# Attention and experts on one core: experts half a step later, order from token lists, value loads first

## The chip, the cores and the metric

One core of one Trainium2 chip. The metric is the time of one execution in microseconds (us), on the device. A kernel is executed several times, its figure is the median, and the profile is of one of those executions; the span that a profile names is 1.6 to 1.7 us shorter than that execution's time. Most executions agree within a per cent; those over 1.5% above the fastest of the same kernel count as slow and stay out of all ratios.

Engine names: PE is TensorE's matmul, PEld its weight load, DVE VectorE, ACT ScalarE, POOL GpSimd, SP the engine that issues most DMA transfers. A bracket such as `[5.14 <-DVE early L464]` says that the engine sat idle for 5.14 us until DVE's work on tile `early` (line 464) was done.

## The reference, cut to what matters

```python
# attention: B=8, H=8, S=576, D=64
s_pos = np.maximum(s, 0.0)
cum = np.cumsum(s_pos, axis=-1)
bias = -(cum[:, :, :, None] - cum[:, :, None, :])          # a decay
scores = np.where(causal, -1e9, scores + np.minimum(bias, 0.0))
attn = softmax(scores);  x = attn @ v                      # (B, S, 512)
# experts: E=8, F=1024, one expert per batch element, top 1
logits = x.mean(axis=1) @ w_gate
e_idx  = np.argmax(logits, axis=1)
h   = np.maximum(x @ w1[e_idx], 0.0)
out = gate_w * (h @ w2[e_idx])
```

The gate needs the mean over all positions of a batch's attention output, and the choice of the expert decides which 2 MB of weights are loaded. So each batch has a chain: last value product, gate matmul, weight load, first expert matmul. The kernel hides it by working on the attention of the next batches meanwhile.

## The kernel before: the parts that matter

A *quad* is four heads of a batch: quads 0 and 1 make batch 0. A *unit* is two heads. Queries and keys come in as fp32, are cast to bf16 on VectorE, transposed on TensorE, and copied out of PSUM by VectorE or ScalarE. GpSimd multiplies the values with the decay.

```python
def cast_qk(n, i):                       # i = 0 query, 1 key (half of the tile)
    src = qk_nat[n][:, i, :, :]
    if n < NEARLY:                       # the first four quads: a plain cast
        qk_bf[n] = early[n]
        nc.vector.tensor_copy(out=qk_bf[n]..., in_=src...)
        return
    ...
    nc.vector.tensor_scalar(             # later quads: the same, and a minimum besides
        out=qk_bf[n]..., in0=src..., scalar1=1.0, scalar2=0.0,
        op0=ALU.mult, op1=ALU.min, accum_out=amin[:, 2*n+i : 2*n+i+1])

def do_vS(n):                            # GpSimd: values times decay
    nc.gpsimd.tensor_tensor(out=dst[:, :, :, 0:D], in0=src, in1=gc..., op=ALU.mult)
    nc.gpsimd.tensor_copy(out=dst[:, :, :, D], in_=gc)
```

The beginning is a hand-written list, the steady part an interleaving computed by budgets:

```python
def begin():
    keep_pe(KEEP0)                       # 11 filler matmuls: keep TensorE's clock up
    cast_qk(0, 0); do_tr_part(0, 0, 0, "a"); do_tr_part(0, 0, 1, "a")
    keep_pe(2); cast_qk(0, 1); ...
    # ... up to the gate of batch 0:
    do_tr_part(3, 0, 0, "v")
    do_vS_pair(2, 0); do_vS_pair(2, 1)   # GpSimd, behind the weight load of batch 0
    load(5, picked[0]); load(6)
    do_scores_masked(4, 0); exp_only(4, 0)
    do_gate2(0)                          # softmax of the gate
    cast_qk(3, 1)                        # VectorE: key of quad 3
    do_tr_part(3, 0, 1, "v"); ...
    do_vS(3)                             # GpSimd again

def emit_all():
    begin()
    for u in range(LAG, END):            # one unit of attention per round
        ...                              # expert quanta placed by weights and budgets
```

## Time and profile before

| | before |
|---|---|
| time, first three runs | 240.71 us median (239.87 to 242.27) |
| span of the profiled run | 240.1 us (that execution took 241.70 us, above the median) |
| first exponential / gate matmul of batch 0 / first expert matmul | 11.5 / 27.1 / 39.4 us |
| starts of the experts of batches 1 to 7 | 63.7, 94.1, 119.8, 146.1, 170.9, 195.1, 216.5 us |
| last expert matmul ends | 233.7 us |

The starts are the times of each batch's first matmul from `xT` and `w_sb` in the timeline. They cut the execution into stretches. Here are VectorE and then GpSimd around 30 us (start, duration, engine, line, operation):

```profile
29.93 0.74 DVE L394 CAST early<-qk_nat 128x1152 bf16<-128x1152 f32 x1
...
31.33 0.24 POOL L454 CAST vS<-g_col 128x10 bf16<-128x10 f32 x1
31.48 1.27 POOL L455 TENSOR_TENSOR vS<-vN,g_col 128x640 bf16<-128x640 f32 x1
```

The cast of quad 3's key takes 0.74 us.

### The profile page before, as it was taken

Reading aid. Unit: us, or ns where it says so; the run is one execution under the profiler, and the core shown is the slowest. Engines: PE = TensorE matmul, PEld = TensorE weight load, DVE = VectorE, ACT = ScalarE, POOL = GpSimd, SP = SyncE. Lnnn points to the kernel's source line nnn. Section 1 sums busy time; section 2 is a strip of 40 time slices with the busy share of each in tenths; the row PEclk is TensorE's granted clock in tenths of the full one; section 3 lists DMA queues with packets and bytes.
Section 4 is the critical chain, followed back from the end, with each engine's and each line's share of the span. In section 5 each row is a group of like instructions: output and inputs, shape, how many; then the busy total and the mean of one; then the engine's idle time right before and its main releaser. Section 6 shows DMA issues by size and latency. Waiting matters only on the chain.

```text
span 240.1 us, 5998 instructions
## 1 busy us (share of the span) xinstructions
PE 214.1 (89%) x2330; PEld 157.1 (65%) x2330; DVE 164.5 (69%) x378; ACT 140.3 (58%) x254; POOL 92.6 (39%) x145
## 2 busy tenths in 40 slices
PE   6597789999999796999899997999999998898990
PEld 2365457875787655867597857776877776557740
DVE  5578768658797784779686875777777544396640
ACT  2588547467656745576648655685658675434330
POOL 6181092018845194308362556218360830100000
PEclk9999859999999999999999999999999999999997
DMA  5999999999999999999999999969921893399222
GB/s 174 342 237 351 306 200 216 344 309 284 221 309 312 286 257 209 304 306 305 225 254 347 313 217 241 337 159 187 228 94 44 162 230 117 67 214 235 82 84 76
DMA packets 55186, 55.14 MB, mean 230 GB/s; under 512 B 39712, under 2 KB 40752, under 8 KB 53104
## 3 DMA queue, kind: packets, MB, share of 16 engines
q1 hardware_dynamic: 52816, 37.91, 51.8%
q0 software_dynamic: 2336, 16.79, 35.4%
q8 instruction: 20, 0.33, 0.5%
q14 instruction: 14, 0.11, 0.2%
HBM read 62.03 MB, written 9.44 MB: 298 GB/s over the span
## 4 chain that ended last, share of the span: by engine, by line
PE 52%; DMA 26%; ACT 7%; DVE 7%; issue 4%; POOLq 1%; SPq 0%; ACTq 0%; POOL 0%; DVEq 0%
DMA w_sb<-in_moe_w_dram 24%; PE mm_ps L655 18%; PE mm_ps L693 13%; PE av_ps L528 6%; PE sc_ps L471 4%; ACT xT L583 4%; PE tr_ps L428 3%; DMA qk_nat<-in_k_dram 2%; ACT pT L501 2%; PE x_ps L580 2%; PE sc_ps L488 1%; PE tr_ps L416 1%; PE lg_ps L617 1%; PE mm_ps L669 1%; POOLq L624 1%
## 5 line engine op out<-in xcount | busy, mean ns | idle before, releaser
L655 PE MATMUL mm_ps<-xT,w_sb 128*128 128x288 bf16 x512 | 74.5, 289 | 4.9 <-DMA w_sb<-in_moe_w_dram 4.4
L501 ACT ACTIVATE pT<-sc_ps 128x1024 bf16<-128x1024 f32 x64 | 62.5, 1021 | 23.5 <-PE sc_ps L471 14.7
L655 PEld LDWEIGHTS <-w_sb 128*128 128x128 bf16 x512 | 61.5, 146 | 9.0 <-DMA w_sb<-in_moe_w_dram 5.1
L693 PE MATMUL mm_ps<-w_sb,hT 128*128 128x512 bf16 x256 | 64.9, 380 | 1.3 <-DMA w_sb<-in_moe_w_dram 0.6
L507 POOL TENSOR_SCALAR_AFFINE_SELECT pT<-pT 128x512 bf16<-128x512 bf16 x50 | 31.5, 638 | 43.8 <-ACT pT L501 43.7
L661 DVE TENSOR_SCALAR hT<-mm_ps 128x288 bf16<-128x288 f32 x64 | 28.7, 454 | 22.0 <-PE mm_ps L655 22.0
L663 ACT ACTIVATE hT<-mm_ps 128x288 bf16<-128x288 f32 x64 | 26.4, 413 | 26.8 <-PE mm_ps L655 26.1
L702 ACT ACTIVATE o_sb<-mm_ps,gw 128x512 f32<-128x512 f32 x32 | 22.1, 691 | 31.2 <-PE mm_ps L693 31.1
L693 PEld LDWEIGHTS <-hT 128*128 128x128 bf16 x256 | 22.8, 98 | 22.1 <-DVE hT L661 2.9
L430 DVE TENSOR_SCALAR_CACHE_REDUCE qkT<-tr_ps 128x1152 bf16<-128x1152 bf16 x24 | 32.5, 1353 | 3.8 <-PE tr_ps L428 3.6
L401 DVE TENSOR_SCALAR_CACHE_REDUCE qk_bf<-qk_nat 128x1152 bf16<-128x1152 f32 x24 | 32.1, 1342 | 0.0
L441 POOL TENSOR_TENSOR vS<-vN,g_col 128x1280 bf16<-128x1280 f32 x13 | 30.3, 2332 | 0.0
L626 POOL DMA_DIRECT2D w_sb<-in_moe_w_dram x8 | 5.2, 645 | 63.1 <-issue 18.7
L528 PEld LDWEIGHTS <-pT 128*128 128x128 bf16 x576 | 22.4, 99 | 4.7 <-ACT pT L501 1.4
L528 PE MATMUL av_ps<-vS,pT 128*128 128x65 bf16 x576 | 23.8, 195 | 1.1 <-ACT pT L501 0.9
L471 PE MATMUL sc_ps<-qkT 64*128 64x256 bf16 (+2 forms) x320 | 21.7, 256 | 1.8 <-ACT qkT L422 1.1
L563 DVE TENSOR_TENSOR x_nat<-av_ps,recip 128x640 bf16<-128x640 f32 x26 | 21.4, 824 | 0.9
L583 ACT ACTIVATE xT<-x_ps 128x576 bf16<-128x576 bf16 x30 | 19.2, 650 | 3.4 <-PE x_ps L580 3.0
L471 PEld LDWEIGHTS <-qkT 64*128 64x128 bf16 x320 | 12.6, 95 | 11.2 <-issue 3.9
L428 PE MATMUL tr_ps<-ident_bf,qk_bf 128*128 128x128 bf16 x216 | 16.0, 219 | 0.1
L428 PEld LDWEIGHTS <-qk_bf 128*128 128x128 bf16 x216 | 13.9, 98 | 3.1 <-DVE qk_bf L401 0.5
L561 DVE RECIPROCAL recip<-av_ps 128x10 f32<-128x10 f32 x26 | 5.7, 220 | 14.0 <-PE av_ps L528 12.9
(92 smaller groups left out, 187.8 us busy)
## 6 DMA issues: line engine op xcount, KB each, us to landing
w_sb<-in_moe_w_dram POOLq DMA_DIRECT2D x16, 1024.0 KB, 12.4
qk_nat<-in_q_dram SPq DMA_DIRECT2D x16, 576.0 KB, 5.6
qk_nat<-in_k_dram SPq DMA_DIRECT2D x16, 576.0 KB, 6.3
vN<-in_v_dram SPq DMA_DIRECT2D x64, 128.0 KB, 5.5
out_dram<-o_sb SPq DMA_DIRECT2D x32, 256.0 KB, 5.7
vN<-in_v_dram SPq DMA_DIRECT2D x16, 64.0 KB, 5.8
out_dram<-o_sb SPq DMA_DIRECT2D x16, 64.0 KB, 4.2
s_nat<-in_s_dram SPq DMA_DIRECT2D x1, 144.0 KB, 2.8
```

Of the source, the lines that this page charges most:

```text
L401: nc.vector.tensor_scalar(out=qk_bf[n][:, i, :, :, :].rearrange("p r hh d -> p hh r d"), in0=src.rearrange("p hh (r d) -> p hh r d", d=D), ...
L428: nc.tensor.transpose(flat[:, r, :], qk_bf[n][:, i, r, :, :], ident_bf)
L430: nc.vector.tensor_scalar(out=tr_out(n, i, 0, R), in0=flat[:, 0:R, :].rearrange("p r (g n) -> p g n r", g=2), scalar1=1.0, scalar2=0.0, op ...
L441: nc.gpsimd.tensor_tensor(out=dst[:, :, :, 0:D], in0=src, in1=gc[:, :, :, None].to_broadcast([P, NT, 4, D]), op=ALU.mult,)
L471: nc.tensor.matmul(sc[:, hh, o : o + W[tj]], src[hh * 64 : hh * 64 + 64, 1, g, tj * P : tj * P + P], src[hh * 64 : hh * 64 + 64, 0, g, tj ...
L501: nc.scalar.activation(out=ph, in_=sc_ps[half], func=AF.Exp, scale=SCALE)
L507: nc.gpsimd.affine_select(out=ap, in_=ap, compare_op=ALU.is_ge, fill=0.0, base=0, pattern=[[0, 4], [1, P]], channel_multiplier=-1,)
L528: nc.tensor.matmul(av[:, ti, :], src[:, o : o + P], vs[:, tj, 2 * hh + u % 2, :], start=(tj == tjs[0]), stop=(tj == tjs[-1]),)
L583: nc.scalar.activation(out=xT[b][:, c, :], in_=flat, func=AF.Copy, accum_out=pooled[b][:, c : c + 1])
L655: nc.tensor.matmul(mm, w1[:, c, ft, :], xT[b][:, c, sc * SC : (sc + 1) * SC], start=(c == 0), stop=(c == NC - 1),)
L661: nc.vector.tensor_scalar_max(out=dst, in0=mm, scalar1=0.0)
L693: nc.tensor.matmul(mm[0:n, :], hT[b][:, fc, st * P : st * P + n], w2[:, fc, :], start=(fc == 0), stop=(fc == NF - 1),)
```

## The change

Its intent: every expert starts half a step later behind its own gate, so that its weights have landed; the order of all engines is no longer computed but read from four lists of tokens, so that it can be tuned place by place; and most value loads of the first quads go out ahead of the later query and key loads.

```diff
+FIRST = """
+L0.0 I L0.1 L1.0 l0.3 l0.1 l3.0 l1.3 l0.0 l1.0 l1.1 L1.1 ...      # loads; I is the load of s
+"""
+BEGIN = """
+k2 C0.0 U0.0.0 u0.0.0.1 U0.0.1 C0.1 J U0.1.0 U0.1.1 ...           # k2: two fillers, were 11
+... g0 C3.1 E4.0 ... U3.1.1 u3.1.1.0 V3 M5.0 ... k6 ... k1 A6 H0.0.1 ...
+... Y0.1.0 V4 x1.3.1 P1.3 H0.1.3 G1 ... m1 ... O0.0 l6.0 L7.0 l7.1 l6.4 y0.1.0 l7.0 ...
+"""
+PERIOD = """
+... P3.1 G3 O1.2 y2.0.0 m3 ... A16 a16 Y2.1.0 T9.1 t9.1 ...       # shifted by i and repeated
+"""
+FINISH = """
+... O7.2 O7.1 Y7.3.0 Y7.3.1 y7.3.1 Z7 y7.4.2 O7.3 D O7.4.2        # D: the guard, now last
+"""
+    def play(text, shift=0):
+        for word in text.split():
+            args = [int(a) for a in word[1:].split(".") if a]
+            if shift:
+                args[0] += shift * STEP[word[0]]
+            ...
+            OPS[word[0]](*args)
 # ... begin(), the budgets and the queue of quanta are gone ...
+    def sum_mm(j):        # N: gate of batch 0 from column sums of the attention output
+        ...
+            nc.tensor.matmul(t, src[0:n, ti, j*P:(j+1)*P], ones_bf[0:n, :], ...)
```

Tokens: `L`/`l` load a query or key / a value part, `C` cast, `U`/`u` transposes of a half and their copy, `T`/`t` the same for a whole one, `J` transposes of the decay, `S`/`M` scores, `E` exponential, `V`/`v` value scaling on GpSimd, `A`/`B` value product, `X`/`x` transposes of the attention output, `G` gate matmul, `m` pick of the expert and weight load, `g` gate softmax, `H`/`h` first expert layer and its output, `Y`/`y` second, `O` store, `k` fillers. The last digit of `u`, `h`, `y` is the engine (0 VectorE, 1 ScalarE). Letters not named here are smaller steps of the same parts.

## The prediction

> **What bounds the kernel now.** I read the page first: the engine shares and the 40 slices.
>
> ```profile
> span 240.1 us, 5998 instructions
> ...
> PE 214.1 (89%) x2330; PEld 157.1 (65%) x2330; DVE 164.5 (69%) x378; ACT 140.3 (58%) x254; POOL 92.6 (39%) x145
> ...
> PEclk9999859999999999999999999999999999999997
> DMA  5999999999999999999999999969921893399222
> ```
>
> TensorE is the fullest engine, but a busy PE slice is not a full PE, so I do not use 89% as the distance to the floor. The clock drops to half near slice 6 (30 to 36 us). The DMA engines are full until about 165 us. Next come the stretches between the starts of the experts of batches 2, 3, 4 and 5, which the chain of waits places at 94.1, 119.8, 146.1 and 171.0:
>
> ```profile
> 20.00:30.00 10.00, 7.17 (x103) 5.15 (x99) 7.64 (x27) 6.80 (x13) 0.33 (x1) 0.92 1.08 325
> 30.00:40.00 10.00, 8.91 (x98) 5.85 (x99) 7.29 (x16) 5.65 (x6) 6.61 (x8) 0.74 1.04 207
> ...
> 94.10:119.80 25.70, 24.64 (x282) 18.71 (x282) 19.33 (x43) 15.66 (x31) 11.34 (x17) 1.00 1.03 278
> 119.80:146.10 26.30, 24.69 (x283) 18.77 (x283) 19.34 (x43) 17.10 (x33) 12.57 (x19) 1.00 1.06 277
> 146.10:171.00 24.90, 24.66 (x283) 18.81 (x284) 19.09 (x42) 15.33 (x31) 11.78 (x18) 1.00 0.93 234
> ```
>
> One batch takes 24.9 to 26.3 us. What it must take I get from the chain of waits, where PE runs back to back:
>
> ```profile
> 71.24 1.73 PE mm_ps L693 x8
> 72.97 0.55 PE sc_ps L471 x10
> ...
> 95.28 0.55 PE av_ps L528 x18
> ...
> 96.84 0.50 PE tr_ps L428 x9
> 97.34 1.97 PE mm_ps L655 x16
> ...
> 109.13 10.65 DMA w_sb<-in_moe_w_dram
> 119.83 1.20 PE mm_ps L655 x8
> ...
> 169.43 0.99 PE mm_ps L669 x16
> ...
> 201.55 0.75 PE x_ps L580 x10
> ...
> 205.17 0.40 PE lg_ps L617 x2
> ```
>
> First expert layer 64 x 1.97/16 = 7.88; second 32 x 1.73/8 = 6.92 and its tail 0.99; scores and values 4 x 0.55 each = 4.4; query and key transposes 4 x 0.50 = 2.0; x transposes 20 x 0.075 = 1.5; gate 0.4. Sum 24.1 us a batch, so the three windows hold 1.6, 2.2 and 0.8 us that no matmul needs. The waits of PE and its weight loads name the cause:
>
> ```profile
> PEld L655 <- DMA w_sb<-in_moe_w_dram: 5.1, 4, 2.2
> ...
> PE lg_ps L617 <- DVE glog L609: 4.5, 4, 1.5
> ...
> PE mm_ps L655 <- DMA w_sb<-in_moe_w_dram: 4.4, 4, 2.1
> ```
>
> (The first and third are largely one wait seen on two rows.) The reader should see that experts start when their weights land, four times up to 2.2 us late, and that the gate matmul sits in PE's queue ahead of ready work.
>
> **The whole span as a sum.** Eight batches are 8 x 24.1 = 192.8. The seven units whose mask is added by matmuls take 1.24 us instead of 0.55 (timeline, 10.76 to 12.00): +4.9. The transposes of the decay column and the guard add about 1. Work 198.7. PE's first useful instruction is at 7.3 us (timeline). Its last ends at about 233.7, 6.4 before the end. So 240.1 - 7.3 - 6.4 - 198.7 leaves 27.7 us of bubble. Where: after 94.1 the work left is six batches, 144.6, less what attention is ahead (8 scores, 6 values, 8 transposes, one x and gate: 4.4 + 3.3 + 4.0 + 1.9 = 13.6), plus guard 0.5 = 131.5, done in 139.6: 8.1 of bubble. The other 19.6 lie before 94.1, about 14 of them before the first expert at 39.4.
>
> **What the Trainium skill says.** (1) "TensorE: Matmul & The Clock Gate", Part 1: the HAM clock gate: an idle window of about 3.4 us halves the clock, a busy one restores it. The trace agrees in kind: after the thin stretch at 20 to 30 the granted clock is 0.74 over 30 to 40. (2) "DMA: Bandwidth & Descriptors", Issuing engines are not separate DMA queues: transfers issued from Sync, Scalar and GpSimd interleave on the same 16 engines. It agrees: weights issued by GpSimd need 8.2 to 15.9 us to land (median 12.4), the long ones while the DMA share is over 1. (3) "Perfetto Trace Analysis", Identifying the Most-Contended Engine: matmul busy share is a poor measure of headroom; hence the issue intervals above. (4) The same page, Optimizing Tensor Performance, Matmuls: rotate groups through PSUM banks so evacuation overlaps the next matmuls. Here four banks rotate, and the chain shows 1.38 us of four ACT records emptying x banks ahead of expert matmuls (at 103.60, 129.35, 155.59).
>
> **The change part by part.** PE arithmetic is almost unchanged: the same matmuls, plus four 5-matmul column sums for batch 0 (about 0.1 us each, an estimate from the per-matmul intervals above: +0.4) and 14 filler matmuls in place of 24, of which the first burst shrinks from 11 to 2.
>
> *Experts later.* In the repeated list the gate matmul of a batch is followed, before that batch's first expert matmul, by 3 scores, 3 values, 2 transposes, 7 first-layer groups, 6 half second-layer groups and a tail: 1.65 + 1.65 + 1.0 + 7 x 0.49 + 6 x 0.865 + 0.99 = 13.9 us of PE work. Before, gate to expert took 13.3 us twice and 13.8 once (106.55 to 119.83, 80.58 to 94.08 and 132.30 to 146.07), with the 1 to 2 us wait inside. So the steady weight wait nearly vanishes: about -1.3 us in each of three periods, -4 in all. For batches 1 and 2 I count only 11.0 and 12.0 us of such work: there a wait of 1 to 2 us stays.
>
> *Order.* The four x transposes are emptied by three ACT and one DVE instruction instead of four ACT ones of 0.65 + 0.20; the gate matmul comes two groups after the transposes. About -0.5 a period. First-layer outputs go 13 to ACT and 3 to DVE (were 8 and 8), second-layer outputs 2 to ACT and 3 to DVE (were 5 and 0). From the rows (0.41 ACT, 0.45 DVE, 0.69 for a wide output) DVE moves by -2.3 + 0.8 + about 2 = +0.5 us a batch, from 19.3 to about 19.9 in 24.6: 81%, not a bound.
>
> *Gate of batch 0.* Column sums straight from the attention output replace the wait for four transposes and their copies. Before: last value output at 23.9, gate matmul at 27.1. After: sums, two small DVE steps, gate matmul at about 25.2. Weights issue about 1.8 us sooner; the softmax no longer sits in front of the key cast on DVE at the same point. First expert at about 37 instead of 39.4, including the half step.
>
> *Loads.* Value loads of the first quads move before the second quad's key. 128 KB of 256 B packets takes 0.59 us of 16 engines (512 packets at the 18.4 ns that the records of the trace give), so seven of them push that key by about 4 us, to about 13.5 to 14.5. Before, its cast ran at 13.86: a draw, with up to 0.8 us of loss.
>
> *Filler.* With 2 instead of 11 matmuls before the first data, PE is probably at half clock at 7.3 us. The first nine to eighteen transposes and the first scores then cost about 1 us more on the path to the first exponential.
>
> *Tail.* The last output is split over two engines and its two stores over two queues, saving one issue of about 0.5 us; the guard's DVE chain, now last, takes about 3 us and lies beside a store that takes over 4. -0.4.
>
> Sum of bubbles: before 94.1, 19.6 - 2 (gate, first expert) - 0.5 (batch 1) - 2.5 (batch 2: 30.4 us between the starts of batches 1 and 2 for 26.6 of work becomes about 28) + 0.5 (cold clock and key not already counted) = 15. After, 8.1 - 4 (weights), with the 0.5 a period for x partly the same time, = 4. Then 7.3 + 199.1 + 19 + 6.0 = 231.4 of span, and the timed median lies 0.6 above the profiled span: about 232. The fine separation of matmuls and evacuations can only take more small waits out; I put **231.5**.
>
> **Rivals.** *DMA becomes the bound.* Summing all packet times of the trace gives 209 us of 16 engines, 26 a batch while everything is loaded: more than PE's 24.1. Shares of 1.03 to 1.06 mean about 24.8 us a batch at best. Against it: no cast waits for a query or key load in the steady state, and loads end near 165 while quad 15 is transposed near 180, so 10 to 15 us are in hand. If it holds, periods stay at 25.5 and the time is 236 to 238. *Cold start costs more than filler saved*: half clock to 14 us or a second drop near 30; the page would lose 2 to 3 us, 234. *Same waits under new names*: strict queues put an evacuation behind one not yet ready and PE meets full PSUM banks; 237 to 241. *A tight order*: bubbles fall to 0.3 a period and the start loses 6 us; 225 to 227.
>
> **Range and chances.** The removable part is 27.7 us; I claim 9. Taking out only the weight waits gives about 236, all tight orders 226. So 225.5 to 238. Faster by over 2% means below 235.9: 0.80. Within 2%: 0.16. Slower: 0.04.
>
> **What would show it.** Right: expert starts of batches 2 to 5 at 24.3 to 25.0 apart; PE waiting on expert weights under 4 us in total, all in batches 0 to 2; gate of batch 0 near 25; first expert near 37; granted clock under 1 in the first 10 us. Wrong: casts or value scaling waiting on loads (DMA bound); PE waits on ACT or DVE evacuation beyond 5 us; a half-clock stretch longer than 7 us; or a last period after attention with PE idle for batch 7's weights, for which I count 11.3 us of cover.

## The result

| | before | after |
|---|---|---|
| time | 240.31 us (239.87 to 242.27, 4 runs) | **248.28 us** (248.12 to 250.79, 4 runs) |
| ratio of fast runs | | 1.034 (1.027 to 1.042) |
| first exponential / fifth | 11.5 / 17.1 | 13.1 / 20.0 |
| gate of batch 0 | 27.1 | 27.6 |
| starts of the experts | 39.4, 63.7, 94.1, 119.8, 146.1, 170.9, 195.1, 216.5 | 46.8, 70.8, 102.5, 127.6, 152.7, 180.8, 204.9, 224.3 |
| last expert matmul ends / span | 233.7 / 240.1 | 240.25 / 249.1 |

Slower by 3.4%, where 3.7% faster was predicted. A ratio here is the mean time of one kernel's fast runs over that of the other's fast runs of the same rounds, so it isn't quite the ratio of the medians.

The profiled execution of after was its slowest; the others had spans of 246.5 to 247.5. Its page:

```profile
span 249.1 us, 5975 instructions
...
PE 214.1 (86%) x2317; PEld 159.4 (64%) x2340; DVE 177.1 (71%) x392; ACT 129.3 (52%) x238; POOL 90.4 (36%) x145
...
PE   2698719899899988999999998699999999899960
...
PEclk9999977999999999999999999999999999999997
DMA  6999999918999699989999999999970794399140
```

TensorE is busy for the same 214.1 us as before in a span 9 us longer. VectorE is busy for 12.6 us more, which is more than the re-dealt outputs explain. There is a hole in PE in slice 6 (31 to 37 us) and one in DMA three slices later (50 to 56 us).

Where do the 9.0 us of the span come from? By the stretches: up to the first expert +7.4; batch 0 to batch 2 +1.0 (55.7 against 54.7); batch 2 to batch 6 +1.4 (102.4 against 101.0); batch 6 to the last expert matmul -3.25 (35.35 against 38.6); the tail +2.45 (8.85 against 6.4). These add up to 9.0. The largest part is one event. VectorE, then GpSimd, then TensorE of after:

```profile
31.28 5.75 DVE L464 CAST early<-qk_nat 128x1152 bf16<-128x1152 f32 x1
```

```profile
31.34 0.24 POOL L549 CAST vS<-g_col 128x10 bf16<-128x10 f32 x1
31.50 1.27 POOL L550 TENSOR_TENSOR vS<-vN,g_col 128x640 bf16<-128x640 f32 x1
...
34.09 2.32 POOL L534 TENSOR_TENSOR vS<-vN,g_col 128x1280 bf16<-128x1280 f32 x1
36.36 0.79 POOL L538 CAST vS<-g_col 128x20 bf16<-128x20 f32 x1
```

```profile
37.08 1.14 PE L491 MATMUL tr_ps<-ident_bf,early 128*128 128x128 bf16 x9 [5.14 <-DVE early L464]
```

The same cast of the same bytes took 5.75 us instead of 0.74, and it took them exactly while GpSimd scaled values. TensorE waited 5.14 us for it, and its clock fell, too (granted share 0.50 from 34.0 to 40.8 us). GpSimd began its values at the same time in both kernels (31.33 and 31.34); the cast came at 29.93 in before and at 31.28 in after.

What the change was made for did work. In the waits of PE and PEld in after there is no row with `DMA w_sb` left, where before had 4.4 and 5.1 us, and the 4.5 us of the gate matmul on `glog` are down to 0.6. But the wait for weights wasn't the same in every execution of the old order. Here is the row of the first expert layer (busy us, mean ns, idle us before it and what ended most of it) in before, then in e3, an experiment below whose steady part is that of before:

```profile
L655 PE MATMUL mm_ps<-xT,w_sb 128*128 128x288 bf16 x512 | 74.5, 289 | 4.9 <-DMA w_sb<-in_moe_w_dram 4.4
```

```profile
L655 PE MATMUL mm_ps<-xT,w_sb 128*128 128x288 bf16 x512 | 74.5, 289 | 2.7 <-DMA w_sb<-in_moe_w_dram 2.2
```

Of the 2.2 us in e3 only 0.2 lie ahead of batches 3 to 5, against 2.2 in before. The steady stretches of after (columns: window, length, then busy us of PE, PEld, DVE, ACT, POOL, then granted clock, DMA share, GB/s):

```profile
70.80:102.50 31.70, 28.38 (x340) 20.93 (x340) 27.27 (x59) 18.15 (x30) 18.28 (x28) 1.00 0.97 252
102.50:127.60 25.10, 24.65 (x285) 18.94 (x285) 19.97 (x43) 15.33 (x32) 11.87 (x19) 1.00 1.02 258
127.60:152.70 25.10, 24.64 (x286) 18.93 (x285) 19.97 (x43) 15.34 (x32) 11.88 (x19) 1.00 1.01 256
152.70:180.80 28.10, 24.84 (x286) 19.00 (x286) 19.97 (x43) 15.48 (x32) 11.92 (x19) 1.00 1.03 261
180.80:204.90 24.10, 23.91 (x275) 18.36 (x275) 14.99 (x35) 15.28 (x32) 9.64 (x17) 1.00 0.65 158
```

25.1, 25.1 and 24.1 are what a period takes in every later run of this order. The 28.1 has one stall of 2.8 us in it, TensorE waiting for an output tile whose store was late. It is in no other profile that follows, and the shorter spans of the other executions fit with its absence.

And this is the same kind of row of before for batch 1 to batch 2, to be held against the first of those:

```profile
63.70:94.10 30.40, 26.56 (x320) 20.23 (x320) 23.22 (x51) 19.93 (x35) 14.54 (x24) 1.00 1.05 275
```

After has 20 matmul records more in this stretch and 1.8 us more of busy PE: the new lists have put more attention work there.

### The profile page after: what moved, and what is told of

Same layout as the page of the kernel before. It is cut to its first block, busy times and chain, and to the rows that moved or that the text cites.

```text
span 249.1 us, 5975 instructions
## 1 busy us (share of the span) xinstructions
PE 214.1 (86%) x2317; PEld 159.4 (64%) x2340; DVE 177.1 (71%) x392; ACT 129.3 (52%) x238; POOL 90.4 (36%) x145
## 4 chain that ended last, share of the span: by engine, by line
PE 63%; DVE 15%; DMA 8%; issue 5%; ACT 4%; POOL 2%; SPq 0%; DVEq 0%; ACTq 0%; POOLq 0%
PE mm_ps L832 21%; PE mm_ps L864 17%; DMA out_dram<-o_sb 6%; PE sc_ps L568 5%; PE av_ps L634 5%; PE tr_ps L512 4%; ACT pT L600 3%; PE x_ps L709 3%; DVE early L464 3%; PE mm_ps L893 2%; DVE qkT L519 2%; DMA s_nat<-in_s_dram 2%; PE sc_ps L585 2%; DVE qk_bf L472 2%; PE tr_ps L491 1%
## 5 line engine op out<-in xcount | busy, mean ns | idle before, releaser
L864 PE MATMUL mm_ps<-w_sb,hT 128*128 128x512 bf16 x235 | 59.7, 379 | 2.7 <-DVE hT L844 0.8
L607 POOL TENSOR_SCALAR_AFFINE_SELECT pT<-pT 128x512 bf16<-128x512 bf16 x50 | 31.4, 637 | 53.2 <-ACT pT L600 49.2
L842 ACT ACTIVATE hT<-mm_ps 128x288 bf16<-128x288 f32 x81 | 30.4, 416 | 29.7 <-PE mm_ps L832 29.2
L864 PEld LDWEIGHTS <-hT 128*128 128x128 bf16 x256 | 23.4, 98 | 24.5 <-issue 2.7
L844 DVE TENSOR_SCALAR hT<-mm_ps 128x288 bf16<-128x288 f32 x47 | 20.5, 452 | 17.4 <-PE mm_ps L832 17.2
L880 ACT ACTIVATE o_sb<-mm_ps,gw 128x512 f32<-128x512 f32 (+1 forms) x24 | 14.6, 624 | 23.9 <-PE mm_ps L864 17.8
L568 PE MATMUL sc_ps<-qkT 64*128 64x256 bf16 (+2 forms) x320 | 22.9, 260 | 3.9 <-DVE qkT L519 1.8
L798 POOL DMA_DIRECT2D w_sb<-in_moe_w_dram x8 | 4.6, 579 | 56.2 <-issue 24.0
L568 PEld LDWEIGHTS <-qkT 64*128 64x128 bf16 x320 | 12.9, 96 | 15.3 <-issue 7.9
L512 PEld LDWEIGHTS <-qk_bf 128*128 128x128 bf16 x216 | 13.9, 98 | 4.7 <-DVE qk_bf L472 1.4
L491 PE MATMUL tr_ps<-ident_bf,early 128*128 128x128 bf16 x72 | 7.8, 266 | 9.1 <-DVE early L464 9.1
## 6 DMA issues: line engine op xcount, KB each, us to landing
w_sb<-in_moe_w_dram POOLq DMA_DIRECT2D x16, 1024.0 KB, 11.7
```

The source lines that it names most:

```text
L512: nc.tensor.transpose(flat[:, r, :], qk_bf[n][:, i, r, :, :], ident_bf)
L568: nc.tensor.matmul(sc[:, hh, o : o + W[tj]], src[hh * 64 : hh * 64 + 64, 1, g, tj * P : tj * P + P], src[hh * 64 : hh * 64 + 64, 0, g, tj ...
L607: nc.gpsimd.affine_select(out=ap, in_=ap, compare_op=ALU.is_ge, fill=0.0, base=0, pattern=[[0, 4], [1, P]], channel_multiplier=-1,)
L842: nc.scalar.activation(out=dst, in_=mm, func=AF.Relu)
L864: nc.tensor.matmul(mm[0:n, :], hT[b][:, fc, st * P : st * P + n], w2[:, fc, :], start=(fc == 0), stop=(fc == NF - 1),)
```

## The experiments

Fourteen kernels ran, all correct. The start of each batch's experts and the first gate are from the profiles (s: the profiled execution was a slow one); the ratio is against before in the same rounds, and a cell is blank where the argument makes no use of it.

| run | what | median us | ratio of fast runs (95%) | gate 0 | first expert | tail |
|---|---|---|---|---|---|---|
| after | the change | 248.28 | 1.034 (1.027 to 1.042) | 27.6 | 46.8 | 8.85 |
| e1 | that cast in the form with a minimum | 245.05 | 1.013 (1.003 to 1.023) | | 41.6 s | |
| e2 | that cast earlier | 245.07 | none, 3 of 4 runs slow | | 42.0 s | |
| e3 | before, that cast later | 240.55 | 1.002 (0.989 to 1.014) | | | |
| e4 | after, guard ahead of the last outputs | 246.27 | 1.027 (1.021 to 1.033) | | | 5.9 |
| e5 | e1, and `V4` behind the gate | 242.86 | 1.010 (1.004 to 1.016) | 27.1 | 40.4 | 9.2 |
| e6 | e5, load order of before | 241.70 | 1.002 (0.997 to 1.007) | | 41.6 | |
| e7 | e5, six outputs to ScalarE | 242.44 | 1.004 (0.999 to 1.010) | | 41.6 | |
| e8 | e5, 11 fillers | 242.31 | 1.006 (1.001 to 1.011) | | 40.4 | |
| e9 | e5, whole start of before | 242.39 | 1.012 (1.008 to 1.016) | 27.7 | 40.9 | |
| e10 | e9, guard as e4, one store moved | 240.49 | 1.003 (1.000 to 1.007) | 27.8 | 41.1 | 6.8 |
| e11 | e5, gate later | 252.34 | 1.054 (1.048 to 1.059) | 27.6 | 40.8 | |
| e12 | before, that cast made to meet GpSimd | 245.55 | 1.024 (1.017 to 1.031) | 26.8 | 44.8 | |
| e13 | e10, first copies as before | 241.13 | 0.996 (0.990 to 1.001) | 24.9 s | 46.2 s | |
| e14 | e13, one value load earlier | 240.09 | 1.003 (0.995 to 1.011) | 28.6 s | 41.8 s | |

### The long cast: e1, e2, e3, e12

My theory after the result: VectorE's plain cast and GpSimd's value scaling exclude each other. The Trainium skill has this on the page "SBUF — State Buffer", section Who interferes with whom: the two engines share a pair of ports, which is an exclusive lock; `copy`, `cast` and `tensor_scalar` can take it, "not the form that also writes out its accumulator". I had not looked it up for the prediction. The rival: the cast waits for something else, a late load or a wrong semaphore order of the new lists.

e1 writes that one cast in the other form, in the same place:

```diff
-            nc.vector.tensor_copy(out=qk_bf[n]..., in_=src...)
+            # only for quad 3, key
+            nc.vector.tensor_scalar(out=qk_bf[n]..., in0=src..., scalar1=1.0, scalar2=0.0,
+                op0=ALU.mult, op1=ALU.min, accum_out=amin[:, 2*n+i : 2*n+i+1])
```

> The changed kernel with one instruction in another form: the cast of the key of quad 3 is a multiply that also writes out its running minimum, as the casts of quads 4 to 15 are; its place in every queue stays. Theory (port lock): the 5.75 us cast at 31.3 was held by GpSimd's run of value scaling from 31.3 to 37.1, because a plain fp32 to bf16 cast takes the port pair that VectorE and GpSimd share; the accumulating form does not, so it takes 1.3 to 1.4 us although GpSimd runs beside it, the first expert moves from 46.8 to about 42 and the time from 248.3 to about 244. Rival (late key): the key of quad 3 had not landed; then the cast still ends near 37 and the time stays at 248. Rival (DMA or clock sets the first expert): the cast gets short, the first expert stays at 46 to 47.

e2 leaves the form and moves the cast ahead of the gate softmax, out of GpSimd's way:

```diff
-... x0.3.0 ... g0 C3.1 E4.0 ...
+... x0.3.0 C3.1 ... g0 E4.0 ...
```

> The changed kernel with one token moved: the cast of the key of quad 3 stands before the softmax of the first gate on VectorE, so it starts near 30.2, ahead of GpSimd's value scaling at 31.3. Theory (port lock): it takes 0.74 us, the first expert moves to about 41 to 42, the time to 243 to 244.5. Rival (late key): the cast waits or ends near 37 as before, time 248.

e3 is the converse in the kernel before: the cast moved behind the transposes that follow it, so that it would fall into GpSimd's stretch.

```diff
         do_gate2(0)
-        cast_qk(3, 1)
         do_tr_part(3, 0, 1, "v")
+        cast_qk(3, 1)
```

> The kernel before with the same cast moved behind the copy of the previous transposes, so that it comes up at about 31.3, as GpSimd's value scaling begins, instead of 29.9. Theory (port lock): if GpSimd is first by a hair, the cast takes 5 to 6 us and the kernel before loses 4 to 5 us (about 245); if VectorE is first, nothing happens (240 to 241). Rivals that put the loss on loads, on the clock or on later experts expect 240 to 241 in either case.

Measured: in e1 the cast took 1.33 us at 32.07, in the middle of GpSimd's work and undisturbed. In e2 it took 0.75 us, ahead of it. Both started the first expert 5 us sooner (41.6 and 42.0). Both profiles are of slow runs; e5 below has e1's cast in a fast one (1.33 us, first expert 40.4). e3 didn't meet its purpose: the cast came early enough to be first (30.26, 0.85 us), so GpSimd's first instruction waited instead (0.65 us where it takes 0.24), and the time didn't change. So I ran a second converse, e12, with a VectorE reduction of 2.5 us, which has to be done some time anyway, put in front of the cast:

```diff
         do_gate2(0)
+        early_max(0)                    # and taken out of the end
         cast_qk(3, 1)
```

> The kernel before with one edit: a reduction of VectorE (2.5 us, needed at the end anyway) moved in front of the cast of the fourth quad's second half, which then starts at about 32.5 instead of 29.9, in the middle of GpSimd's value scaling (31.3 to 36.6). Theory (the two engines exclude each other): the cast takes 4 us or more instead of 0.74, and ends with GpSimd's work at about 36.5 to 37; the first expert matmul moves from 39.4 to about 43 to 45. Rival (the long cast of the changed kernel was due to the order of its loads or something else of that kernel): the cast takes 0.75 to 0.9 us wherever it is put, the first expert matmul moves by 2 us or less.

VectorE of e12, in the kernel before:

```profile
29.91 2.53 DVE L792 TENSOR_REDUCE amax<-early 128x1 f32<-128x2304 bf16 x1
32.36 3.76 DVE L394 CAST early<-qk_nat 128x1152 bf16<-128x1152 f32 x1
```

and GpSimd:

```profile
31.96 1.25 POOL L455 TENSOR_TENSOR vS<-vN,g_col 128x640 bf16<-128x640 f32 x1
33.18 2.32 POOL L441 TENSOR_TENSOR vS<-vN,g_col 128x1280 bf16<-128x1280 f32 x1
35.45 0.79 POOL L445 CAST vS<-g_col 128x20 bf16<-128x20 f32 x1
```

The cast took 3.76 us instead of 0.74, the first expert moved from 39.4 to 44.8, and the kernel before became 2.4% slower (1.7 to 3.1) by one instruction moved. About 2.5 of those 5.4 us are the reduction's own length in front of the cast and about 3.0 the lock; the split is rough, because TensorE's granted clock over 34 to 41 us was 0.50 here and 0.91 in before. The rival falls: no load and no list of the changed kernel is in e12. Both ways round, the form of the instruction and who comes first decide. (The wait shows in the duration of the cast, not as idle time ahead of it, so no view of waits on VectorE names it; only TensorE's wait for `early` does.)

### The second lock: e5

e1 moved the first expert by 5.2 us and the time by about 2%, which is as much. Its timeline has another collision. VectorE, GpSimd, and TensorE of e1 near 52 us (this profile is of a slow run):

```profile
51.72 2.49 DVE L756 SCALAR_TENSOR_TENSOR glog<-w_gate_sb,pooled,glog 128x8 f32<-128x8 f32 x2
```

```profile
51.53 2.33 POOL L543 TENSOR_TENSOR vS<-vN,g_col 128x1280 bf16<-128x1280 f32 x1 [8.64 <-PE mm_ps L841]
```

A sum over 8 columns, 0.23 us elsewhere, took over 2 us of those 2.49 (in e2, also a slow run, 1.88). It reads two operands from SBUF, and GpSimd was reading its own there. The gate of batch 1 hangs on it. e5 moves that value scaling behind the pick of the expert:

```diff
-... Y0.1.0 V4 x1.3.1 P1.3 H0.1.3 G1 H0.1.1 h0.1.1.0 m1 h0.1.3.0 ...
+... Y0.1.0 x1.3.1 P1.3 H0.1.3 G1 H0.1.1 h0.1.1.0 m1 V4 h0.1.3.0 ...
```

> The changed kernel with the accumulating cast and, beside it, GpSimd's value scaling of quad 4 moved behind the pick of the second gate. In the run with the cast alone, that scaling (51.5 to 53.9) ran beside a gate step on VectorE that reads two SBUF operands, which took 2.2 us instead of 0.23; PE idled 1.7 us for it and its clock then dropped to half over 54 to 58. Theory (port lock again): all gate steps take 0.2 to 0.25 us, no half clock there, the second batch's experts start at 65 to 67 instead of 68.9, time 241.5 to 243.5. Rival (weights of batch 1 or attention order set that start): it stays at 68 to 69 and the time at 244 to 245.

First expert 40.4, batch 1 at 64.4, batch 2 at 96.1, then periods of 25.1, 25.1, 25.1 and 24.1; 242.86 us. All sums of the second gate are at 0.22 to 0.23 us again, and batch 0 to batch 1 takes 24.0 us, where e1 needed 27.3. From the gate of batch 0 to its first expert after needed 19.2 us, e1 13.9 and e5 13.3: the first collision, with the half clock that came with it, accounts for 5.3 to 5.9 us of the 9, and the ratio went from 1.034 to 1.010. (e5 shares no rounds with after; both are held against before.) The second collision has no part in the 9: in after GpSimd was done with quad 4 at 53.8, the sums ran from 54.2 on at 0.22 to 0.23 us each, and batch 0 to batch 1 took 24.0 us, too. It came up only once the first was gone, and whether e5 gained anything over e1 the fast runs don't show (1.010, 1.004 to 1.016, against 1.013, 1.003 to 1.023). What remains is a start that is still late, a stretch of 31.7 us where I predicted 28, and the tail.

### The tail: e4

```diff
-... O7.2 O7.1 Y7.3.0 Y7.3.1 y7.3.1 Z7 y7.4.2 O7.3 D O7.4.2
+... O7.2 O7.1 D Y7.3.0 Y7.3.1 y7.3.1 Z7 y7.4.1 O7.3 O7.4.2
```

> The changed kernel with the guard moved ahead of the last wide output, as the kernel before has it, and the last output on one engine with both stores from Sync. Theory: the guard's chain on VectorE and what follows it now end the kernel; from the last matmul of the experts to the end goes from 8.8 back to about 6.4 us, the time from 248.3 to about 246. Rival: the store of the last output ends it in both; then at most 0.5 us.

The end of after, VectorE alone, shows why:

```profile
240.78 0.49 DVE L878 TENSOR_SCALAR o_sb<-mm_ps,gw 64x256 f32<-64x256 f32 x1 [4.50 <-ACT o_sb L877]
...
243.64 0.20 DVE L120 TENSOR_SCALAR gd_bad<-gd_ok 1x1 uint32<-1x1 f32 x1
```

The last output had been split in two to save time, but its second half waited for the first (0.5 us), and only then did VectorE start on the guard, a flag that all engines read before the program ends. The execution ends 5.3 us after that flag. In e4 the tail from the last expert matmul to the end is 5.9 us instead of 8.85, and the ratio falls from 1.034 to 1.027. (e4 moves the guard and leaves the last output on one engine; the two aren't told apart.)

### The half step itself: e11

In the repeated list the gate matmul and the pick come one quad's transposes later; the experts stay where they are.

```diff
-... P3.1 G3 O1.2 y2.0.0 m3 l11.2 ... A16 a16 Y2.1.0 T9.1 t9.1 l12.1 ...
+... P3.1 O1.2 y2.0.0 l11.2 ... A16 a16 Y2.1.0 T9.1 t9.1 G3 m3 l12.1 ...
```

> e5 with one edit: in the repeated period (batches 3 to 6) the gate matmul and the pick of the expert come one quad's transposes later, some 4 us later in the TensorE order (at 135.3 instead of 131.4 in the first of the periods), so the weight load is asked for later and the experts keep their place. Theory (the half step between gate and experts is what removed the weight waits): the weights took 11.1 us from issue to landing and had about 1 us to spare, so TensorE waits for the weights again, 2 to 3 us in each of four periods; the periods become 27 to 28 us instead of 25.1, time 250 to 254. Rival (the waits had gone for another reason, for example since the loads of values and keys no longer stand in front of the weights): no weight wait, periods 25.1, time 243.

```profile
PE mm_ps L840 <- DMA w_sb<-in_moe_w_dram: 4.3, 4, 1.6
...
PE mm_ps L840 <- ACT hT L850: 2.0, 4, 0.5
```

The wait for weights is back, and the periods became 27.5, 28.0, 26.6 and 26.8 us. 252.34 us, 9.5 us above e5 in these four periods together. So in the new order it is the distance of gate and expert that keeps the waits away, and not the order of the loads. The listed waits account for some 6 of the 9.5; the rest I can't place by rows.

### The stretch from batch 1 to batch 2: e7, and part of e10

e7 gave six of batch 1's first-layer outputs from VectorE to ScalarE (VectorE's 27.3 us in 31.7 looked like a bound).

```diff
-h1.0.1.0 h1.0.3.0 h1.0.5.0 h1.0.7.0 h1.1.2.0 h1.1.6.0
+h1.0.1.1 h1.0.3.1 h1.0.5.1 h1.0.7.1 h1.1.2.1 h1.1.6.1
```

> As the run with both locks taken out, with six of batch 1's first-layer outputs moved from VectorE to ScalarE. Theory: between the starts of batches 1 and 2 VectorE is the bound (93% busy over 20 us, the chain runs through its casts and copies), so taking 6 x 0.45 us from it shortens that stretch from 31.8 to about 30 us and the time by 1 to 2 us. Rival (late loads behind the stores on Sync set the casts there): the stretch stays within 0.5 us.

A miss: the stretch stayed at 31.8 us. e10 (below) also moved the first output store behind five loads that it blocked in the DMA queue (`O0.0 l6.0 L7.0 l7.1 l6.4 y0.1.0 l7.0` to `l6.0 L7.0 l7.1 l6.4 y0.1.0 l7.0 O0.0`). The stretch is still 31.4. The hole in the DMA share near 50 us was gone before that edit (0.12 over 50 to 55 us in after, 1.05 in e5, whose stretch is 31.7). So neither VectorE nor that hole sets it. In e10 PE is busy for 28.5 of 31.4 us and the longest of its waits there is 0.8 us: it is work, put there by the list, with small waits on top. From batch 0 to batch 2 e10 needs 55.7 us and before 54.7.

### The start: e6, e8, e9, e10, e13, e14

e6 took the load order of before (`I L0.0 L0.1 L1.0 L1.1 l0.0 l0.1 ...`), e8 the fillers (`k2` to `k11`), both on e5.

> As the run with both locks taken out, with the first 26 loads in the order of the kernel before (s first, then queries and keys of two quads, then values): undoes the load part of the change alone. Theory: s lands near 3.8 instead of 6.1, the decay column no longer holds PE from 7.2 to 9.0, the first exponential starts at 12 or before instead of 13.1, and 1 us is left of it at the first expert (40.5 to 41). Rival (values first pays): the value scaling waits for loads again and the first expert comes no earlier, or later than 41.6.

> As the run with both locks taken out, with 11 filler matmuls at the start as in the kernel before. Theory: PE is at full clock from the first transposes on; nine transposes take 0.50 us instead of 0.96 and the first exponential starts 0.4 to 0.8 us sooner; the first expert 0 to 0.5 us sooner, since ScalarE's exponentials set that stretch, and the time is the same within 0.5 us. Rival (the cold start is a main part of the loss): 1.5 us or more.

Neither helped the start much: first exponential 12.8 and 12.9 (13.4 in e5), first expert 41.6 and 40.4 (40.4). The fast runs of e6 are 0.9 us below those of the same rounds of e5 (means 241.8 and 242.7), which its profile, its slowest run, doesn't explain. e9 did both, and put the transposes of the decay where before has them (`J U0.1.0 U0.1.1` to `U0.1.0 J U0.1.1`). e10 added the guard edit and the store edit.

> The changed kernel with both locks avoided (as in e5) and the whole start set back to that of before: the first load order, nine more filler matmuls ahead of the first transposes, and the decay-column transposes behind the third group of key transposes instead of ahead of it. Each of the first two alone gave nothing (e6, e8). Theory 1 (the start is one chain of small delays: a cold TensorE clock without the fillers, and the wait for the decay columns with them; each hides the other): first exponential 11.5 (e5: about 13), fifth about 17 (e5: about 20), first gate 24.5 to 25.5, first expert matmul 38 to 39 instead of 40.4, time 240 or a little less. Rival (the start has slack up to the first gate, which is bounded by the value scaling and the second quad's loads): first gate still near 27, first expert at 40 to 41, time 242 to 243.

> e9 with two more edits: the guard's work put ahead of the last output groups instead of behind them (as in e4), and the first output store issued behind the five loads that it stood in front of in the DMA queue. Theory: the guard edit takes 1 to 2.5 us off the tail (e4: the tail after the last expert matmul 5.9 instead of 8.85); the store edit closes the hole in the DMA share of 46 to 55 us, and if that hole is what makes the stretch from the second to the third batch's first expert matmul 31.7 us long, the stretch falls to 29 to 30. Together 236 to 239, below both kernels. Rival (the stretch is bound by something else): stretch still 31.5 to 32, time about 1.5 below e9.

e9 fell: first gate 27.7, first expert 40.9, and TensorE again at half clock from 9.6 to 16.4 us. e10 gained 1.9 us over e9, about what the guard edit promised, and equals before (ratio 1.003). e13 gave the copies of the first key groups to the engines that before uses, and put two fillers between the query and the key of quad 0:

```diff
-k11 C0.0 U0.0.0 u0.0.0.1 U0.0.1 C0.1 U0.1.0 J U0.1.1 u0.0.1.0 u0.1.0.0 u0.1.1.1 k1 M0.0 ...
+k11 C0.0 U0.0.0 u0.0.0.1 U0.0.1 u0.0.1.1 k2 C0.1 U0.1.0 u0.1.0.0 J U0.1.1 u0.1.1.1 M0.0 ...
-U1.0.0 u1.0.0.1 U1.0.1 M1.0 E1.0 C1.1 u1.0.1.0 k1 ...
+U1.0.0 u1.0.0.0 U1.0.1 u1.0.1.0 k1 M1.0 E1.0 C1.1 k1 ...
```

> e10 with the copies of the first two key groups given to the engines and the order of before: the second and fourth key group of quad 0 to ScalarE again, one group of quad 0 alone to VectorE, both groups of quad 1's first half to VectorE, so that no copy stands between the first four exponentials on ScalarE; and two fillers between the first key's halves, as before. In e10 VectorE had the decay columns (10.80 to 11.27) and then two copies of 0.71 in a row, and the scores waited for the second until 12.38. Theory (the start is late because of this chain of copies, not the loads or fillers): first exponential 11.5 to 12.0 instead of 14.0, fifth 17 to 18 instead of 20.2, first gate 25 to 26 instead of 27.8, first expert matmul 38.5 to 39.5 instead of 41.1, time 1.5 to 2.5 below e10: 238 to 239.5, ratio 0.992 to 0.998. Rival (the value scaling on GpSimd or the later keys set the first gate): first exponential earlier, fifth still near 20, first gate over 27, time as e10 (240.5).

Its start was as expected: first exponential 11.65, fifth 17.3, gate 24.9. But the profiled execution, a slow one, lost all of it at once:

```profile
42.62 2.33 POOL L543 TENSOR_TENSOR vS<-vN,g_col 128x1280 bf16<-128x1280 f32 x1 [11.19 <-DMA vN<-in_v_dram]
```

The earlier gate had sent 2 MB of weights out 0.4 us behind the last value load of quad 3, TensorE waited 8.3 us for those values, and the first expert came at 46.2. The seven executions had spans from 236.2 to 245.2. e14 moved that load ahead (`l3.2 l3.3 L4.0 L4.1 ... m0 l3.4` to `l3.2 l3.3 l3.4 L4.0 L4.1 ... m0`).

> e13 with one edit: the last value load of quad 3 asked for in front of quad 4's query and key loads instead of behind them. In e13's profile the gate came at 24.9, so the 2 MB of weights were asked for 0.4 us after that load (3.7 us after it in e10); the load, behind 1.15 MB in its own queue and beside the weights, came late, GpSimd started quad 3's values at 42.62, and TensorE waited 8.3 us for them, all in the executions of 240 us and more. Theory (the earlier start only lost a race between that value load and the weights): the wait is gone in all executions, the first expert matmul at 38 to 39, spans of 235.5 to 237.5 in all runs, time 237 to 239, ratio 0.983 to 0.992: below both kernels. Rival (DMA has no room for an earlier start: what comes first pushes back something else): another load is late, for example the key of quad 4, PE waits 3 us or more for a cast or a value, time 239 to 242.

e14 had spans from 235.7 to 239.6, none like e13's worst two, which fits its theory but doesn't prove it, because the profiled execution, a slow one again, didn't start early: first exponential 13.8, gate 28.6. Its list up to there is that of e13, copies and fillers included. What differs is the speed of TensorE. The first transposes in e13, then in e14:

```profile
7.25 0.68 PE L500 MATMUL tr_ps<-ident_bf,early 128*128 128x128 bf16 x9 [1.27 <-DVE early L473]
```

```profile
8.03 1.14 PE L500 MATMUL tr_ps<-ident_bf,early 128*128 128x128 bf16 x9 [1.68 <-DVE early L473]
```

Nine transposes take 0.68 us at full clock and 1.14 at half (in e10, where the granted clock over 10 to 16 us is 0.50, they take 1.15). So the copies weren't the cause, or not most of it: e10, without them and at half clock soon after, had its first exponential at 14.0, e14 with them at 13.8. The page "TensorE: Matmul & The Clock Gate" of the Trainium skill (Part 1: the HAM clock gate) says that the clock is set from activity in a free-running window, so that one and the same kernel can find it in another phase. The profiles agree: the profiles of before, e3 and e12, which share before's start, are at full clock here; the eight with two fillers (after, e1, e2, e4, e5, e6, e7, e11) are all at half clock; with eleven fillers e8, e9 and e10 began at full clock and fell to half at the next wait, e13 kept it, and e14 did not have it. The clock records in the packed traces agree: the first return to full clock is at 4.5 us in before, 6.3 in e3, 7.0 in e12 and 5.5 in e13, but at 16.9 in after and 17.6 in e14; e10 is at full clock from 5.8 to 9.2 and again from 16.0. The first exponential is at 11.2 to 11.7 where full clock lasts through the start and at 12.8 to 14.0 in the other twelve. That the clock is what delays it is argued from this, not tested alone. A start with fillers is better, but it looks like a matter of luck in each execution (in e14 the data landed 0.8 us later than in e13, 7.2 against 6.4); no run shows how often it holds.

No version beat both kernels. e10, e13 and e14 are within 0.5% of before.

## Why the prediction was wrong, point by point

**The step that failed: "the softmax no longer sits in front of the key cast on DVE at the same point. First expert at about 37 instead of 39.4."** The cast was taken to cost its 0.74 us wherever it stands. In the new place it met GpSimd's value scaling and cost 5.75. I had misread the list, too: `g0`, the softmax, still stands directly in front of `C3.1`, and the cast came 1.35 us later than before (31.28 against 29.93), not sooner. I had counted busy time per engine and semaphore waits, and the two engines have no semaphore between them. The first expert came at 46.8; with the collision taken out at 40.4 (e5). All rivals that I named kept the engines independent, so none contained this; the one of a cold start came true beside it (below).

**Gate of batch 0: "gate matmul at about 25.2".** Measured 27.6, and the weights were issued at 30.2, 0.5 us later than before and not 1.8 sooner. The column sums do save what I said, but the attention arrives late: the fifth exponential is 2.9 us later than before. This is the term *Filler* mis-sized, "about 1 us more", and *Loads*, "a draw, with up to 0.8 us of loss": the half clock lasts to 16.9 us, so a sign of being wrong that I had named, a half-clock stretch longer than 7 us, came true. In e13's profile, at full clock, the gate came at 24.9, so the saving itself was right by 0.3 us.

**Batch 2: "30.4 us between the starts of batches 1 and 2 for 26.6 of work becomes about 28".** Measured 31.7. I took the 26.6 us of work from the stretch of before. The lists put 28.4 us of busy PE there. That could be counted from the tokens, and I counted only the part between gate and expert.

**Weight waits: "nearly vanishes: about -1.3 us in each of three periods, -4 in all".** Right in the cause (no wait left in after and e5; e11 brings it back) and wrong in size: three periods took 76.8 us before and 75.3 in e5, -1.5. (From gate to expert before took 13.3, 13.5 and 13.8 us, not 13.3 twice.) And most of what I meant to save belonged to one execution: my profile of before took 241.70 us, above the median, and in e3 and e12, with the same steady order, these three periods take 74.8 us with 0.2 us of wait for weights. Against those e5 is 0.5 us longer. The floor of 24.1 us per batch was too low, too. In e10's period from 121.9 to 147.0 the listed wait of PE is 0.3 us and it still takes 25.1. At nine of the 29 places where one kind of matmul follows another, the next start is 0.10 to 0.19 us later than within a group, 1.2 us together; at the other twenty there is no such delay, and why at these nine isn't shown. These handovers were in the "bubbles" that I meant to remove. And for batches 1 and 2, where I expected a wait of 1 to 2 us to stay, there is none.

**Tail: "-0.4".** Measured +2.45. I took the guard's chain to lie beside the last store, but the program's end waits for its flag, and the split of the last output was in series. e4 took 2.95 us of it back.

**The share of DVE, "81%, not a bound"** held: 19.97 of 25.10 us in the steady period, 80%. **The rival of a DMA bound** can be dropped for the steady part: shares of 1.01 to 1.06 at 25.1 us a period and no load waited for there. In the start it is real (e13). **After batch 6** the change gained 3.25 us, more than I had allotted, since more of the attention is done by then; it is part of what the earlier stretch pays.

What stays open: why e11's periods grew by more than the listed waits, what the wait for weights of the old order depends on, and whether the start can be held at full clock in every execution.

## What to carry to other kernels

When an order is changed, ask not only which engine waits for which, but which instructions will run at the same moment on engines that share something; a plain cast on VectorE beside work of GpSimd is such a pair, and on VectorE a duration that grows is its only trace. Count the work in each stretch of the new order before subtracting a wait from the old one, and take the floor of a stretch from one that runs without waits. Look for the wait that you want to remove in a second profile of the old kernel: here most of it was gone there. Take single profiles of the first 15 us as one draw: whether the clock is up can differ between executions of the same list.

## What the Trainium skill lacked or had wrong

- "SBUF — State Buffer", two separate sides and Who interferes with whom: right on who collides (cast 0.74 to 5.75 us; 1.33 us beside GpSimd in the form with an accumulator; a sum with two operands from SBUF 0.23 to over 2 us; GpSimd's first instruction 0.24 to 0.65 us where the cast was first, e3). It says that the pair is held for a whole instruction. Lacking: instructions of GpSimd that follow each other at once can keep it. In after the cast outlasted five of them in a row, from 31.34 to 36.4, and was let in ahead of the sixth (0.79 us instead of 0.27); in e12 it was passed over once, at 33.2.
- "TensorE: Matmul & The Clock Gate", Part 1: the free-running window agrees with e13 and e14. The page warns that clock events in a trace have been seen to be unreliable; here they agree with the durations, and it is our view that misleads. Its granted clock over 5 to 16 us reads 1.00 in after and in e14 while nine transposes take 1.14 instead of 0.68 us, because it counts time ahead of the first clock record (16.9 and 17.6 us) as full. There the durations tell it.
- The time that a handover from one kind of matmul to another costs: none of the pages has a figure for it; here 0.10 to 0.19 us at nine of 29 places in 25.1 us.
